# Seven half products for block 1's second product, with loads and neighbouring work moved

## The chip, the cores and the metric

The kernel runs on one core of one Trainium2 chip. A core has TensorE (PE in the profile; PEld is its weight load), VectorE (DVE), ScalarE (ACT), GpSimd (POOL) and SyncE (SP, which here only issues DMAs). Each engine runs its own instructions in program order and waits by semaphores for the others; SP, ACT and POOL can issue DMAs, in their own order too. The metric is the device time of one execution in microseconds (us); before the change the median of three runs is 279.38 us.

## What is computed

Linear attention over 8 batches, 8 heads, 576 positions and a head dimension of 64, with an RMS norm per head, and behind it a layer norm and a two-layer perceptron with a residual (512 to 2048 to 512):

```python
kv = np.einsum('bhsd,bhse->bhde', k, v)
out = np.einsum('bhsd,bhde->bhse', q, kv)
rms = np.sqrt(np.mean(out * out, axis=-1, keepdims=True) + 1e-06)
x = out / rms * g_norm                      # heads side by side: 512 columns
...
xn = (x - mu) / np.sqrt(var + 1e-06) * g_ln
ch = np.maximum(xn @ w_ch1, 0.0) @ w_ch2
return (x + ch).astype(np.float32)
```

Inputs and output are float32, the matrix products run in bfloat16.

## The kernel before

**Blocks and tiles.** Of each batch's 576 positions, 512 make one block of four tiles of 128 rows; the 64 left of each batch are gathered in a ninth block, "rem". For a block PE makes the first product (`mm1`, into `m1`, with ACT's ReLU from a PSUM bank of tag "p1", of which there are three) and then the second (`mm2`), which is scaled by the row's 1/std (`rstds`) and added to x. Blocks follow one another on PE without a break: mm1 and mm2 of block 0, of block 1, and so on.

**The attention of the next batch** is made in between. For batch b: `kv_of(b)` (40 small matmuls into the one PSUM bank of tag "misc", then two ACT copies); the turning of q, either by a DVE copy into `q_p` and a DMA transpose issued by SP (`turn_q_dma`), or in part by PE transposes through "misc" or "ops" banks and ACT copies (`turn_q`); and four tiles. `plan_tile` puts a tile's steps at given times: `first` is the product o (PE), its square (ACT) and the reduction over heads (DVE); `second` is the root (ACT), its inverse, y, x and the centred bfloat16 copy xc (all DVE); `turn` transposes xc, on PE (through "misc", with an ACT copy) or by a DMA transpose; `var` is the sum of squares on ACT.

**Time by hand.** `tick()` is called by the products, about once per 16 matmuls of 128 columns or 4 of 512, and runs what `at(slot, fn)` has put on the agenda for that tick, before the matmuls of the tick. So a slot sets the place of an instruction in the order of each engine's queue, not a time. A block has 16 ticks of mm1 and 16 of mm2, or 14 of mm2 if it is in `SEVEN`; slots are counted at 32 a block, and those in the second half of a block of `SEVEN` are pressed together by 14/16.

**Seven half products.** In the blocks of `SEVEN` (2 to 7 and "rem") `mm2_seven` makes the second product by Strassen's scheme in Winograd's form: rows, the 2048 inner elements (even and odd groups) and the columns are each halved, and seven products of halves with sums of halves take the place of eight. The sums of the weights' quarters, T1 to T4, are made once by DVE (slots 40 to 43); those of m1's quarters, S1 to S4, are made by DVE in each block as the ReLUs come in (`row_sums`), S3 in place. Each product is two ticks of eight matmuls with 256 columns. ACT scales results out of PSUM, DVE adds others (L558), and POOL adds float32 halves, x among them. Block 2 alone has its own order of products, and its mm1 handles two tiles at a time (256 columns); later blocks take four (512 columns).

**Blocks 0 and 1** make the second product straight, in 64 matmuls of 512 columns (L697). Block 0's is cut into parts of the inner dimension, because w2 is still arriving; for both, `finish` scales and adds by one DVE operation per tile (L706), and `store` issues the tile's two DMAs on SP (on POOL for tiles 2 and 3 of block 1). Block 1's mm1 runs tile by tile (128 columns).

**Loads** are issued by POOL, in program order: w1, w2[0:4] and [4:8] (128 rows each), batch 1's q, k and v in two DMAs each, the rest of w2, then, from slot 9.6, memsets and batch 2's k, v and q. The loads of a later batch reuse the buffers of the one before the last; POOL first copies one element of the turned q (`gate`), which makes it wait until that q has been read.

Of the kernel before, what the change touches and what calls it, by code (L numbers as in the profile page):

```python
# [14 lines left out]
def kernel(  # L15
# [11 lines left out]
    nc = tc.nc  # L27
# [19 lines left out]
    NB = 2  # L47
# [124 lines left out]
    load_w2(0, 4)  # L172
    load_w2(4, 8)
    for dst, src in ((q_in, q), (k_in, k), (v_in, v)):
        load(dst[1], src, 1)
    load_w2(8, 10)
    load_w2(10, 12)
    load_w2(12, nDe)

# [270 lines left out]

    def plan_tile(s, make, turn_at, on_pe, var_at):
        box = []

        def first():
            t = make()
            box.append(t)
            if t.mms:
                t.o()
            t.sq()
            t.red()  # L460

        def second():
            t = box[0]
            t.y()
            t.x()
            t.xc_w()

        at(s, first)
        at(s + 2, second)
        at(turn_at, lambda: box[0].turn(on_pe))  # L470
        at(var_at, lambda: box[0].var())
# [8 lines left out]

    SEVEN = {2, 3, 4, 5, 6, 7, "rem"}
    H2, C2 = nDe // 2, Dm // 2
    SPLIT = (0, 6, 12, nDe)
    SPLIT_2, TICKS_2 = (0, 12, nDe), ((0, 1, 4, 7), (0, 1, 4, 6))
    sums = {}

# [3 lines left out]
    def w2_q(odd, cols):  # L490
        return w2_sb[:, odd::2, cols * C2:cols * C2 + C2]

    B11, B12, B21, B22 = (w2_q(o, c) for o, c in ((0, 0), (0, 1), (1, 0), (1, 1)))
    weight_sums = (lambda: nc.vector.tensor_sub(T1, B12, B11),
                   lambda: nc.vector.tensor_sub(T3, B22, B12),
                   lambda: nc.vector.tensor_add(T2, T3, B11),
                   lambda: nc.vector.tensor_sub(T4, B21, T2))

# [40 lines left out]
    def mm2_seven(b):  # L539
# [22 lines left out]
        def p1():  # L562
            product(p_x, a11, b11, True, False)
            scaled(v0, p_x, 0)
            scaled(v1, p_x, 1)

        def p2():
            product(p_x, a12, b21, False, True)
            scaled(o(0, 0), p_x, 0)
            G.tensor_add(o(0, 0), o(0, 0), x(0, 0))  # L570

# [7 lines left out]
        def p4():  # L579
            product(p_q, a22, T4, True, True)  # L580
            scaled(q, p_q, 1)
            G.tensor_add(q, q, x(1, 0))  # L582

        def p5():
            product(p_z, S1, T1, True, False)
            scaled(r5, p_z, 1)
            G.tensor_add(r5, r5, x(1, 1))

        def p6():
            product(p_y, S2, T2, True, False)  # L590
            scaled_add(u2, p_y, 0, v0)
            G.tensor_add(u2, u2, x(0, 1))

        def p7():
# [3 lines left out]

        for p in ((p1, p4, p2, p5, p6, p7, p3) if b == 2 else (p1, p4, p6, p5, p2, p3, p7)):
            p()  # L600
# [64 lines left out]
    def mm1(b, t0, n, c0=0, c1=nDe):  # L665
# [3 lines left out]
        for de0 in range(c0, c1, per):  # L669
            tick()  # L670
            p1 = ps1.tile([128, per, n * 128], f32, tag="p1", name="p1")
            for i in range(per):
                de = de0 + i
                for kk in range(nK):
                    nc.tensor.matmul(p1[:, i, :], lhsT=w1_sb[:, kk, de * 128:(de + 1) * 128],  # L675
                                     rhs=blk[2][:, kk, sl],
                                     start=(kk == 0), stop=(kk == nK - 1))
            nc.scalar.activation(m1[:, de0:de0 + per, sl], p1, func=AF.Relu)  # L678
            del p1
            if b == 2 and t0 + n == 4 and de0 + per in SPLIT_2:  # L680
                i = SPLIT_2.index(de0 + per)
                row_sums(b, SPLIT_2[i - 1] // 2, SPLIT_2[i] // 2, TICKS_2[i - 1])
            elif b in SEVEN and b != 2 and de0 + 1 in SPLIT:
                i = SPLIT.index(de0 + 1)
                row_sums(b, SPLIT[i - 1] // 2, SPLIT[i] // 2, range(4))
# [16 lines left out]
    def finish(b, ts, p2):  # L702
        if ts % 2 == 0:
            o_pair[b] = outp.tile([128, 2, Dm], f32, tag="osb", name="o_sb")
        o_sb = o_pair[b][:, ts % 2]
        nc.vector.scalar_tensor_tensor(o_sb, in0=p2, scalar=rstds[b][:, ts:ts + 1],  # L706
                                       in1=blks[b][0][:, ts], op0=ALU.mult, op1=ALU.add)
        store(b, ts, o_pair[b][:, ts % 2:ts % 2 + 1])

    def store(b, ts, o_sb, c0=0, c1=Dm, upper=None):  # L710

        n = o_sb.shape[1]
        if b == "rem":
# [4 lines left out]
            return  # L718
        eng = nc.gpsimd if b == 1 and ts >= 2 else nc.sync
        for half in range(2):  # L720
# [155 lines left out]
    at(9.5, next_memsets)  # L876
    load_batches(9.6, (("k", 2), ("v", 2), ("q", 2)), lambda: ())
    at(11, lambda: t[3].turn(True))
# [4 lines left out]

    def q_start():
        q_ps[1] = kv_in.tile([128, JJ, H, D], bf16, tag="qp", bufs=1, name="q_p")
        nc.vector.tensor_copy(q_ps[1].rearrange("p j h d -> p h j d"), q_in[1])
        qts[1] = qt_pool.tile([128, JJ, HP, 128], bf16, tag="qt", name="qt")
        nc.sync.dma_start_transpose(
            qts[1][:, 2:].rearrange("p j hp t -> p (j hp) t"),
            q_ps[1][:, 2:].rearrange("p j h d -> p (j h d)"))  # L890

    def q_turns():
        turn_q(1, 0, ps_out, "ops")
        turn_q(1, 1, ps_m, "misc")
        del q_ps[1]

    at(14.5, q_start)
    at(19, q_turns)
    at(23, lambda: kv_of(1))
    for j, s, tn in ((0, 24, 30), (1, 27, 34), (2, 31, 38), (3, 35, 42)):  # L900
        plan_tile(s, lambda j=j: main_tile(1, j), tn, True, s + 6.7)
    at(36.2, lambda: keep_q(1))
    at(46, lambda: rstd_of(1))

    at(36, lambda: kv_of(2))
    at(36.9, lambda: turn_q_dma(2))
    for j, s, tn in ((0, 45, 51), (1, 49, 55), (2, 53, 61), (3, 57.5, 63)):
        plan_tile(s, lambda j=j: main_tile(2, j), tn, False, s + 6.7)
    at(58, lambda: keep_q(2))
    at(70, lambda: rstd_of(2))  # L910

# [4 lines left out]
    for slot, what, after in (  # L916
            (47, (("k", 3), ("v", 3), ("q", 3)), lambda: (turned_q(2),)),
            (68, (("q", 4), ("k", 4), ("v", 4)),
             lambda: (turned_q(3), blks[2][2][:1, nK - 1, 511:])),
            (92.7, (("q", 5), ("k", 5), ("v", 5)), lambda: (turned_q(4),)),  # L920
# [4 lines left out]

    for b, s in ((3, 56), (4, 93), (5, 123), (6, 155), (7, 187)):
        at(s, lambda b=b: kv_of(b))
# [14 lines left out]

    for b, at_q, at_o in ((3, 56.2, (66.9, 70.7, 74.5, 78.4)), (4, 81, (96.5, 102.7, 109, 115)),
                          *((b, 32 * b - 47.2, tuple(32 * b - i for i in (34.5, 27.3, 20.1, 12.9)))
# [6 lines left out]
    for i in range(nK):  # L951
        at(17 + i, lambda i=i: nc.vector.tensor_scalar_mul(w1_sb[:, i], w1_sb[:, i],
                                                           g_lnT_sb[:, i:i + 1]))
    for i, fn in enumerate(weight_sums):
        at(40 + i, fn)

# [5 lines left out]
    p2s += [ps2.tile([128, Dm], f32, tag="p2", name="p2") for _ in range(2)]  # L962
    for de0, de1 in ((0, 8), (8, 10), (10, 12)):
        for ts in range(4):
            mm2_part(0, ts, p2s[ts], de0, de1)
    for ts in range(4):
        p2 = p2s[ts]
        p2s[ts] = None
        mm2_part(0, ts, p2, nDe * 3 // 4, nDe)
        finish(0, ts, p2)  # L970
        del p2
    del blks[0], m1s[0]
    for ts in range(4):
        mm1(1, ts, 1)
    mm2(1)
# [38 lines left out]
```

## Time and profile before

| | us |
|---|---|
| median of 3 runs (279.3 to 279.63) | 279.38 |
| the profiled execution | 279.33 |
| its span, first to last instruction | 277.3 |
| PE busy | 269.2 |
| DVE busy | 195.9 |
| ACT busy | 179.5 |
| POOL busy | 101.7 |

The order of the first stages, by the first matmul of each in the chain of waits: block 0's mm1 at 14.83, its mm2 at 32.60, block 1's mm2 at 65.05, block 2's mm1 at 80.39, block 3's mm1 at 109.59; and in the timeline block 1's mm1 at 48.48 and block 2's mm2 at 95.14. From 150 to 200 PE is busy for all of the 50 us, and DVE for 35.6. In the chain of work that ended last PE has 82% of the span, DVE 8%, DMA 4%.

How to read the lines shown below: a line of the chain is start, duration, engine, operation and source line, with the number of instructions merged; a line of a timeline is the same with the shapes, and in brackets how long the engine stood idle before it and what released it; a line of waits is who waited for whom, the total, how often, and the longest. A window's line is start and end, and then for each engine the busy time and the number of instructions.

### The profile page before, as it was taken

What the parts mean: (1) busy time and instruction counts of PE and PEld (TensorE: products, weight loads), DVE (VectorE), ACT (ScalarE), POOL (GpSimd) and SP (SyncE); (2) the same over time, 40 slices, a digit from 0 to 9 for tenths busy, and PEclk for the clock granted to TensorE, in tenths of its full rate; (3) what the DMA queues carried; (4) which work ended last, traced back from release to release, by engine and by line L of the source; (5) the groups of instructions that cost most, each with busy time, mean ns of one, the idle gap of its engine ahead of it and who ended that gap; (6) DMA issues with size and microseconds to landing.
All of it is one profiled execution on the core that took longest, in us unless ns stands there. A gap on an engine that the chain in (4) does not pass through costs nothing.

```text
span 277.3 us, 6629 instructions
## 1 busy us (share of the span) xinstructions
PE 269.2 (97%) x2614; PEld 189.6 (68%) x2614; DVE 195.9 (71%) x446; ACT 179.5 (65%) x398; POOL 101.7 (37%) x127
## 2 busy tenths in 40 slices
PE   8899999999999999999999999999999999999994
PEld 3589855996569886458845874597458745874683
DVE  6676438897966898899569856985797469923564
ACT  3567754796448783777677767776777487846610
POOL 8522770025034256701870187017201800180141
PEclk9999999999999999999999999999999999999999
DMA  7999999959995994995499639991611061105032
GB/s 215 199 207 205 200 197 190 260 106 144 189 183 84 199 126 92 216 227 98 41 185 239 134 26 178 245 134 21 161 28 21 20 163 29 21 20 151 2 76 76
DMA packets 65366, 36.80 MB, mean 133 GB/s; under 512 B 35120, under 2 KB 62004, under 8 KB 65336
## 3 DMA queue, kind: packets, MB, share of 16 engines
q0 software_dynamic: 28736, 18.29, 46.4%
q1 hardware_dynamic: 36008, 17.12, 30.4%
q10 hardware_dynamic: 592, 0.98, 1.0%
q8 instruction: 20, 0.33, 0.5%
q14 instruction: 10, 0.08, 0.1%
HBM read 36.71 MB, written 9.44 MB: 166 GB/s over the span
## 4 chain that ended last, share of the span: by engine, by line
PE 82%; DVE 8%; DMA 4%; ACT 3%; issue 1%; POOL 1%; DVEq 0%; POOLq 0%
PE p L675 42%; PE p L697 8%; PE p_y L519 7%; PE p_z L519 7%; PE p_x L519 6%; PE p_s L519 4%; DMA w_sb<-in_moe_w_ch_dram 4%; PE p_q L519 3%; PE o_ps L298 2%; PE kv_ps L271 2%; DVE S L509 1%; DVE ss L375 1%; DVE x_blk L397 1%; DVE o_ps L379 1%; DVE S L508 1%
## 5 line engine op out<-in xcount | busy, mean ns | idle before, releaser
L675 PE MATMUL p<-xT_blk,w_sb 128*128 128x128 bf16 (+2 forms) x1024 | 131.5, 286 | 0.6 <-DMA w_sb<-in_moe_w_ch_dram 0.4
L678 ACT ACTIVATE m<-p 128x512 bf16<-128x512 f32 x144 | 85.5, 597 | 38.9 <-PE p L675 36.2
L675 PEld LDWEIGHTS <-w_sb 128*128 128x128 bf16 x1024 | 78.7, 98 | 45.0 <-issue 0.7
L519 PEld LDWEIGHTS <-m 128*128 128x128 bf16 x448 | 43.3, 98 | 6.5
L375 DVE TENSOR_REDUCE ss<-sq 128x8 f32<-128x512 f32 x35 | 23.8, 680 | 28.7 <-ACT sq L304 28.6
L582 POOL TENSOR_TENSOR q<-q,x_blk 128x512 f32<-128x512 f32 x6 | 8.1, 1348 | 83.1 <-ACT q L553 83.1
L519 PEld LDWEIGHTS <-S 128*128 128x128 bf16 x344 | 32.8, 98 | 4.8 <-DVE S L509 1.1
L697 PE MATMUL p<-w_sb,m 128*128 128x512 bf16 x128 | 29.6, 379 | 0.0
L415 ACT ACTIVATE dev<-x_blk,st_blk 128x512 f32<-128x512 f32 x36 | 25.8, 718 | 1.4 <-DVE st_blk L401 1.4
L379 DVE TENSOR_TENSOR o_ps<-o_ps,inv 128x512 f32<-128x512 f32 x33 | 23.1, 700 | 3.1
L304 ACT ACTIVATE sq<-o_ps 128x512 f32<-128x512 f32 x35 | 20.8, 595 | 5.0 <-PE o_ps L298 5.0
L397 DVE SCALAR_TENSOR_TENSOR x_blk<-o_ps,g_norm_sb 128x512 f32<-128x512 f32 x33 | 22.8, 691 | 1.1
L519 PE MATMUL p_x<-w_sb,m 128*128 128x256 bf16 x192 | 23.4, 273 | 0.0
L697 PEld LDWEIGHTS <-m 128*128 128x128 bf16 x128 | 12.0, 98 | 12.3
L383 ACT ACTIVATE rms<-ss,eps_sb 128x8 f32<-128x8 f32 x36 | 10.7, 297 | 12.6 <-DVE ss L375 12.2
L507 DVE TENSOR_TENSOR S<-m 128x768 bf16<-128x768 bf16 (+2 forms) x20 | 10.7, 536 | 11.4 <-ACT m L678 11.4
L422 DVE TENSOR_SCALAR xc<-x_blk,st_blk 128x512 bf16<-128x512 f32 x32 | 17.7, 553 | 1.1
L558 DVE SCALAR_TENSOR_TENSOR u<-p_y,rstd,v 128x256 f32<-128x256 f32 x24 | 10.4, 476 | 5.0 <-PE p_y L519 5.0
L509 DVE TENSOR_TENSOR S<-m,S 128x768 bf16<-128x768 bf16 (+2 forms) x20 | 12.6, 634 | 0.4
L553 ACT ACTIVATE v<-p_x,rstd 128x256 f32<-128x256 f32 x24 | 9.4, 475 | 5.0 <-PE p_x L519 5.0
L390 DVE RECIPROCAL inv<-rms 128x8 f32<-128x8 f32 x36 | 7.1, 197 | 7.6 <-ACT rms L383 7.3
L519 PE MATMUL p_z<-w_sb,S 128*128 128x256 bf16 x96 | 11.8, 273 | 0.6 <-DVE S L509 0.6
(143 smaller groups left out, 347.6 us busy)
## 6 DMA issues: line engine op xcount, KB each, us to landing
out_dram<-o_sb SPq DMA_DIRECT2D x24, 256.0 KB, 6.1
w_sb<-in_moe_w_ch_dram POOLq DMA_DIRECT2D x7, 512.0 KB, 13.5
q_in<-in_q_dram POOLq DMA_DIRECT2D x7, 320.0 KB, 5.2
k_in<-in_k_dram POOLq DMA_DIRECT2D x7, 320.0 KB, 7.8
v_in<-in_v_dram POOLq DMA_DIRECT2D x7, 320.0 KB, 11.1
q_in<-in_q_dram POOLq DMA_DIRECT2D x8, 256.0 KB, 8.2
out_dram<-o_sb SPq DMA_DIRECT2D x16, 128.0 KB, 4.6
k_in<-in_k_dram POOLq DMA_DIRECT2D x7, 256.0 KB, 8.7
```

The source lines that it names most:

```text
L304: nc.scalar.activation(self.sq_t, self.o_ps, func=AF.Square)
L375: nc.vector.tensor_reduce(self.ss, self.sq_t, axis=AX.X, op=ALU.add)
L379: nc.vector.tensor_mul(self.o_ps, self.o_ps, self.inv().to_broadcast([128, H, D]))
L383: nc.scalar.activation(self.r, self.ss, func=AF.Sqrt, scale=1.0 / D, bias=eps_sb)
L397: nc.vector.scalar_tensor_tensor(x_blk[:, ts].rearrange("p (h d) -> p h d", h=H), in0=self.o_ps, scalar=1.0, in1=g_norm_sb.to_broadcast([1 ...
L415: nc.scalar.activation(dev, x_blk[:, ts], func=AF.Square, bias=st[:, 1, ts:ts + 1], accum_out=st[:, 2, ts:ts + 1])
L422: nc.vector.tensor_scalar_add(self.xc_t, x_blk[:, self.ts], st[:, 1, self.ts:self.ts + 1])
L509: lambda: nc.vector.tensor_sub(S4, a12, S2),
L519: nc.tensor.matmul(dst[:, t - ts[0], :c1 - c0], lhsT=a[:, i, t * 128:(t + 1) * 128], rhs=w[:, i, c0:c1], start=start and t == ts[0] and i ...
L675: nc.tensor.matmul(p1[:, i, :], lhsT=w1_sb[:, kk, de * 128:(de + 1) * 128], rhs=blk[2][:, kk, sl], start=(kk == 0), stop=(kk == nK - 1))
L678: nc.scalar.activation(m1[:, de0:de0 + per, sl], p1, func=AF.Relu)
L697: nc.tensor.matmul(p2[:, c0:c1], lhsT=m1s[b][:, de, ts * 128:(ts + 1) * 128], rhs=w2_sb[:, de, c0:c1], start=(de == 0), stop=(de == nDe - 1))
```

## The change

Block 1 joins `SEVEN`, with block 2's order of products and two-tile groups for its tiles 2 and 3 in mm1. In blocks 1 and 2 three of POOL's additions are put behind that of u2. Block 1's row sums get their own ticks.

The weights' sums are cut into four calls of four operations on 512 columns, one at slot 13 and three at 34.5 to 39. w2 is loaded in pairs behind w2[0:4], and batch 1's q and k go ahead of them, its v behind the first pair; block 0's parts follow the pairs. Batch 2's q is loaded ahead of its k and v. Block 0's outputs are scaled by ACT and added by POOL, and their stores are issued by POOL at slot 40.2. Batch 1's attention steps come one to three slots earlier, batch 2's q is partly turned on PE, its tile 3 too, and slots of batches 2 and 3 and the loads of 3 and 4 move; batch 4's loads no longer wait for block 2's last transposed tile.

```diff
     load_w2(0, 4)
-    load_w2(4, 8)
-    for dst, src in ((q_in, q), (k_in, k), (v_in, v)):
-        load(dst[1], src, 1)
-    load_w2(8, 10)
-    load_w2(10, 12)
-    load_w2(12, nDe)
+    load(q_in[1], q, 1)
+    load(k_in[1], k, 1)
+    load_w2(4, 6)
+    load(v_in[1], v, 1)
+    for de in range(6, nDe, 2):
+        load_w2(de, de + 2)
...
-    def plan_tile(s, make, turn_at, on_pe, var_at):
+    def plan_tile(s, make, turn_at, on_pe, var_at, second_at=None):
...
-        at(s + 2, second)
+        at(second_at or s + 2, second)
...
-    SEVEN = {2, 3, 4, 5, 6, 7, "rem"}
+    SEVEN = {1, 2, 3, 4, 5, 6, 7, "rem"}
...
+    TICKS_1 = ((1, 2, 4, 7), (0, 1, 2, 5))
...
-    weight_sums = (lambda: nc.vector.tensor_sub(T1, B12, B11),
-                   lambda: nc.vector.tensor_sub(T3, B22, B12),
-                   lambda: nc.vector.tensor_add(T2, T3, B11),
-                   lambda: nc.vector.tensor_sub(T4, B21, T2))
+    def weight_sums(i0, i1):
+        i = slice(i0, i1)
+        t1, t2, t3, t4, b11, b12, b21, b22 = (w[:, i] for w in (T1, T2, T3, T4, B11, B12, B21, B22))
+        nc.vector.tensor_sub(t3, b22, b12)
+        nc.vector.tensor_add(t2, t3, b11)
+        nc.vector.tensor_sub(t4, b21, t2)
+        nc.vector.tensor_sub(t1, b12, b11)
...
+        late = []
+
+        def add(dst, a, c):
+            if b in (1, 2):
+                late.append(lambda: G.tensor_add(dst, a, c))
+            else:
+                G.tensor_add(dst, a, c)
...
-            G.tensor_add(o(0, 0), o(0, 0), x(0, 0))
+            add(o(0, 0), o(0, 0), x(0, 0))
...
-            G.tensor_add(q, q, x(1, 0))
+            add(q, q, x(1, 0))
...
-            G.tensor_add(r5, r5, x(1, 1))
+            add(r5, r5, x(1, 1))
...
             G.tensor_add(u2, u2, x(0, 1))
+            while late:
+                late.pop(1 if len(late) == 3 else 0)()
...
-        for p in ((p1, p4, p2, p5, p6, p7, p3) if b == 2 else (p1, p4, p6, p5, p2, p3, p7)):
+        for p in ((p1, p4, p2, p5, p6, p7, p3) if b in (1, 2) else (p1, p4, p6, p5, p2, p3, p7)):
...
-            if b == 2 and t0 + n == 4 and de0 + per in SPLIT_2:
+            if b in (1, 2) and t0 + n == 4 and de0 + per in SPLIT_2:
                 i = SPLIT_2.index(de0 + per)
-                row_sums(b, SPLIT_2[i - 1] // 2, SPLIT_2[i] // 2, TICKS_2[i - 1])
-            elif b in SEVEN and b != 2 and de0 + 1 in SPLIT:
+                row_sums(b, SPLIT_2[i - 1] // 2, SPLIT_2[i] // 2, (TICKS_1 if b == 1 else TICKS_2)[i - 1])
+            elif b in SEVEN and b not in (1, 2) and de0 + 1 in SPLIT:
...
-        nc.vector.scalar_tensor_tensor(o_sb, in0=p2, scalar=rstds[b][:, ts:ts + 1],
-                                       in1=blks[b][0][:, ts], op0=ALU.mult, op1=ALU.add)
-        store(b, ts, o_pair[b][:, ts % 2:ts % 2 + 1])
+        r, x = rstds[b][:, ts:ts + 1], blks[b][0][:, ts]
+        nc.scalar.activation(o_sb, p2, func=AF.Copy, scale=r)
+        nc.gpsimd.tensor_add(o_sb, o_sb, x)
+        o_tile = o_pair[b][:, ts % 2:ts % 2 + 1]
+        at(40.2, lambda: store(b, ts, o_tile))
...
-        eng = nc.gpsimd if b == 1 and ts >= 2 else nc.sync
+        eng = nc.gpsimd if b == 0 or b == 1 and ts >= 2 else nc.sync
...
-    load_batches(9.6, (("k", 2), ("v", 2), ("q", 2)), lambda: ())
+    load_batches(9.6, (("q", 2), ("k", 2), ("v", 2)), lambda: ())
...
-    at(14.5, q_start)
-    at(19, q_turns)
-    at(23, lambda: kv_of(1))
-    for j, s, tn in ((0, 24, 30), (1, 27, 34), (2, 31, 38), (3, 35, 42)):
-        plan_tile(s, lambda j=j: main_tile(1, j), tn, True, s + 6.7)
-    at(36.2, lambda: keep_q(1))
+    at(12.5, lambda: q_start(1, 2))
+    at(17, lambda: q_turns(1, (ps_out, "ops"), (ps_m, "misc")))
+    at(22, lambda: kv_of(1))
+    for j, s, tn in ((0, 23, 28.6), (1, 26, 33), (2, 29, 37), (3, 32, 39)):
+        plan_tile(s, lambda j=j: main_tile(1, j), tn, True, (27.7, 41, 43, 45)[j])
+    at(33.2, lambda: keep_q(1))
...
-    at(36, lambda: kv_of(2))
-    at(36.9, lambda: turn_q_dma(2))
-    for j, s, tn in ((0, 45, 51), (1, 49, 55), (2, 53, 61), (3, 57.5, 63)):
-        plan_tile(s, lambda j=j: main_tile(2, j), tn, False, s + 6.7)
-    at(58, lambda: keep_q(2))
-    at(70, lambda: rstd_of(2))
+    at(40, lambda: kv_of(2))
+    at(29.5, lambda: q_start(2, 1))
+    at(35, lambda: q_turns(2, (ps_m, "misc")))
+    for j, s, x_at, tn, va in ((0, 42, 44, 46, 55.5), (1, 44.2, 46.2, 49, 57.5),
+                               (2, 55.5, 59.5, 61, 63), (3, 60.5, 62.6, 70, 67.5)):
+        plan_tile(s, lambda j=j: main_tile(2, j), tn, j == 3, va, x_at)
+    at(61, lambda: keep_q(2))
+    at(70.5, lambda: rstd_of(2))
...
-            (47, (("k", 3), ("v", 3), ("q", 3)), lambda: (turned_q(2),)),
-            (68, (("q", 4), ("k", 4), ("v", 4)),
-             lambda: (turned_q(3), blks[2][2][:1, nK - 1, 511:])),
+            (43, (("q", 3), ("k", 3), ("v", 3)), lambda: (turned_q(2),)),
+            (61.5, (("q", 4), ("k", 4), ("v", 4)), lambda: (turned_q(3),)),
...
-    for b, s in ((3, 56), (4, 93), (5, 123), (6, 155), (7, 187)):
+    for b, s in ((3, 62.5), (4, 93), (5, 123), (6, 155), (7, 187)):
...
-    for b, at_q, at_o in ((3, 56.2, (66.9, 70.7, 74.5, 78.4)), (4, 81, (96.5, 102.7, 109, 115)),
+    for b, at_q, at_o in ((3, 52, (68.5, 72.5, 76.5, 83)), (4, 81, (96.5, 102.7, 109, 115)),
...
-    for i, fn in enumerate(weight_sums):
-        at(40 + i, fn)
+    for i0, i1, slot in ((0, 2, 13), (2, 4, 34.5), (4, 6, 37), (6, 8, 39)):
+        at(slot, lambda i0=i0, i1=i1: weight_sums(i0, i1))
...
-    for de0, de1 in ((0, 8), (8, 10), (10, 12)):
+    for de0, de1 in ((0, 4), (4, 6), (6, 8), (8, 10), (10, 12), (12, 14)):
         for ts in range(4):
             mm2_part(0, ts, p2s[ts], de0, de1)
...
-        mm2_part(0, ts, p2, nDe * 3 // 4, nDe)
+        mm2_part(0, ts, p2, 14, nDe)
         finish(0, ts, p2)
...
-    for ts in range(4):
-        mm1(1, ts, 1)
+    mm1(1, 0, 1)
+    mm1(1, 1, 1)
+    mm1(1, 2, 2)
     mm2(1)
```

`q_start(b, j0)` and `q_turns(b, ...)` are the old `q_start` and `q_turns` with the batch as an argument: `q_start` copies q to `q_p` on DVE and turns the groups from j0 on by a DMA transpose, `q_turns` turns the others on PE.

## Prediction

> **What bounds the kernel now.** I read the page's busy times first, then the waits of PE, the chain of waits, the busy times by stretches of five microseconds, and the timelines of DVE, ACT and POOL around block 1.
>
> ```profile
> PE 269.2 (97%) x2614; PEld 189.6 (68%) x2614; DVE 195.9 (71%) x446; ACT 179.5 (65%) x398; POOL 101.7 (37%) x127
> ```
>
> PE is busy for 97%, and the slices show its clock at 9 throughout. What PE no longer has to do is gained, unless PE then waits. It waits very little now:
>
> ```profile
> PE p_z L519 <- DVE S L509: 0.6, 1, 0.6
> PE p L675 <- DMA w_sb<-in_moe_w_ch_dram: 0.4, 1, 0.4
> ```
>
> The first of these is block 2's seventh row sum. In the chain:
>
> ```profile
> 102.07 3.36 DVE S L509 x2
> 105.43 0.04 issue
> 105.47 0.39 PE p_z L519 x2
> 105.87 0.75 PE kv_ps L271 x40
> ```
>
> The other side is DVE around block 1 (columns PE, PEld, DVE, ACT, POOL, clock, DMA share, GB/s; of 5 us each): 4.86, 4.17 and 4.68 are busy, ACT up to 4.84, and POOL is idle.
>
> ```profile
> 45.00:50.00 5.00, 5.00 (x51) 3.34 (x50) 4.86 (x11) 2.52 (x6) 0.40 (x1) 1.00 1.42 194
> 50.00:55.00 5.00, 4.93 (x115) 4.82 (x113) 4.17 (x10) 4.41 (x12) 0.00 (x0) 1.00 1.25 287
> 55.00:60.00 5.00, 5.00 (x93) 5.00 (x91) 4.68 (x9) 4.84 (x12) 0.00 (x0) 1.00 0.68 143
> ```
>
> **PE's own sum.** Second product of block 1: the chain has 28 matmuls of L697 in 6.04 us, 0.216 each, 64 make 13.80. A half product (16 of L519) is 1.75 us, seven make 12.25: **-1.55**. First product: row groups 2 and 3 go together. 64 matmuls of 128 columns take 3.57 us (0.0558 each), 32 of 256 columns 3.49 (0.109): 128 of the one, 7.14, become 64 of the other, 6.98: **-0.16**. Added: four transposes for q of batch 2 and four for its tile 3, 0.22 each (L429 x4): **+0.44**. The o products and kv products only move. Block 2's wait: **-0.58**, see below. Sum **-1.85**.
>
> **Loads.** In the timeline of POOL every load issue waits for the landing of the eighth load before it:
>
> ```profile
> 23.43 0.68 POOL L98 DMA_DIRECT2D v_in<-in_v_dram  x1 [1.94 <-DMA w_sb<-in_moe_w_ch_dram]
> 25.95 0.71 POOL L119 DMA_DIRECT2D w_sb<-in_moe_w_ch_dram  x1 [1.84 <-DMA w_sb<-in_moe_w_ch_dram]
> 28.44 0.71 POOL L119 DMA_DIRECT2D w_sb<-in_moe_w_ch_dram  x1 [1.78 <-DMA w_sb<-in_moe_w_ch_dram]
> 30.26 0.76 POOL L119 DMA_DIRECT2D w_sb<-in_moe_w_ch_dram  x1 [1.11 <-DMA q_in<-in_q_dram]
> ```
>
> So the last quarter of w1 landed at 23.4, w2[0:4] at 25.9, w2[4:8] at 28.4: 512 KB per 2.55 us. In the new order that rate gives q1 28.8, k1 31.7, w2[4:6] 32.9, v1 35.8, w2[6:8] 37.1, then each pair 1.27 later, the last at 42.2. Needs, with tick 16 at 32.60 (first L697), 0.8625 a tick and what lies between: w2[4:6] 36.5, v1 38.2 (tick 22), w2[6:8] 39.0, w2[8:10] 40.9. The thinnest slack is 1.9 us; I take 0. Gone, it costs what is late, one for one; the bound is -0 to +1, as qt's transpose (4.37 us on SP) shares the DMA engines. Two more w2 issues (0.75 each) put POOL's memsets and batch 2's six issues 1.4 us later, to 36.4; q2, now first of them, lands at 45, k2 and v2 by 51 (kv of batch 2 is at 57). The eight stores of block 0 leave SP, which has only transposes there, for POOL: 0.54 each (1.63 for three in block 1), 4.3 us from tick 40 (56.7). Batch 3's gate stands behind them at 61.2, against 61.0 now. Batch 4's gate comes at 75 instead of 83, so its copy waits for nothing.
>
> **DVE.** Block 0's outputs (L706, 0.74, every 0.66) leave it: -2.6 us before 51.4. The weight sums become 16 operations of 512 columns: such a row sum takes 0.42 and the next starts 0.45 later, so 1.8 us a call; four calls 7.2 instead of 4 x 1.24 = 5.0. The first call is at tick 13, where DVE idles now (4.21 us), the others after tile 3 of batch 1. Block 1's row sums add 0.87 and 0.33 (spacings in the chain) four times, 4.8 us, and six L558 of 0.43 replace four L706. So DVE has no gap between 44 and 74:
>
> Tile 1 of batch 1 ends its xc at 48.78 now. Its tile 0 comes a tick (0.86) earlier and one L706 less stands before it: 47.75. Reduce of tile 2, 0.65: 48.4. Copy of q2, 0.82: 49.2. Inverse to xc of tile 2, 2.4 (46.40 to 48.78 for tile 1 now): 51.6. Reduce of tile 3: 52.25. ACT's root behind it, 0.30, stands in ACT's queue at tick 34 ahead of the ReLUs of ticks 34 on and the copy of q2's transposes; with 0.60 and 0.57 these end at 53.7. PE wants the one "misc" bank again at tick 37: 32.60 + 16 x 0.8625 + 5 x 0.89 + 0.45 + 0.75 + seven times 0.22 = 53.6. So there is **no slack left**: what delays DVE between 48 and 53 delays PE one for one, through ACT. Behind it, the last part of S1 would end at 70.1, and the product that reads it starts at 70.3; S2, S4 and S3 have 2 us and more. At the end of block 1, POOL's six additions (1.27 each) now run beside the xc of batch 2's tiles 2 and 3. With one wait of 0.75 for each of these the last ends at 83.7, and PE turns it at tick 68, 84.7: nothing reaches PE; without that slack, up to +0.7.
>
> **ACT and POOL for block 0's outputs.** ACT gets four copies (0.60) at 47.4 to 49.9, two of them behind tile 2's root. Three of batch 1's variances (0.71) leave the ticks up to 40 for 41 to 45, which makes up for them, and the ten scalings of block 1's halves (0.475) fall in ticks without a ReLU: 0 for ACT by itself; were PE to wait for one such copy, +0.6. POOL gets four additions of 1.27 to 1.35 (L582, L575) from about 48.0 to 53.2. This is where a price is unknown:
>
> ```profile
> 112.89 1.34 POOL L575 TENSOR_TENSOR o_sb<-u,q 128x512 f32<-128x512 f32 x1
> 114.12 1.33 POOL L576 TENSOR_TENSOR o_sb<-u,r 128x512 f32<-128x512 f32 x1
> 114.14 1.61 DVE L422 TENSOR_SCALAR xc<-x_blk,st_blk 128x512 bf16<-128x512 f32 x1
> 31.29 2.35 DVE L886 COPY q_p<-q_in 128x2560 bf16<-128x2560 bf16 x1 [4.21 <-DMA q_in<-in_q_dram]
> ```
>
> xc has a median of 0.49, here it takes 1.61 under POOL additions: +1.12. The copy of q takes 0.82, under POOL's memsets 2.35. No row has the copy under an addition. In the new order it is ready at 48.4 and the first addition starts at 48.0. Two DVE operations can meet POOL there: the copy (to 49.3, +0.9) and tile 2's xc (+0.75, the rest of the third addition). Bounds: 0 if DVE comes first, 1.65 with both. A small lead of either engine decides, so I take one wait of the middle size, **+0.85**. The Trainium skill ("SBUF — State Buffer", section "Who interferes with whom") says that DVE and GpSimd share a port pair as an exclusive lock and that whoever issues first blocks the other for the whole instruction. By that rule both would wait here, and the sum would be -0.2; the trace has it for xc, not for the copy.
>
> **Block 2.** Its row sums ran beside POOL's additions (L508 on 512 columns 1.49 instead of 0.42, the two L509 3.42 instead of 0.87 + 0.33). These additions now come after u's, when the sums are done; also u's no longer stands behind three others. Tile 3 of batch 3 comes later, and adds about 3 us to DVE there. From tick 76 the sums and tiles need 7.9 us to the end of S4, which is read 12 ticks (10.5 us) later; the wait of 0.58 goes. If not, +0.58.
>
> Total: -1.85 + 0.85 = **-1.0**. The profiled execution took 279.33 with a span of 277.3, so 2.03 lie around it; the median is 279.38. I predict 276.3 for the span and **278.4** for the median.
>
> **Rivals.** (1) DVE gets in ahead of POOL, or the waits end in slack: 279.38 - 1.85 = 277.5. For it: the two are 0.4 us apart; against: POOL is busy for five microseconds without a break. (2) Both waits count in full: -0.2, 279.2. (3) DVE's unbroken stretch is the bound: S1's last part comes a microsecond late, because the copy of q3 or the weight sums are slowed, and the fourth product waits: 279.4. For it: 0.2 us of slack; against: PE's stalls before it widen that slack. (4) **Slower**: q2 lands late. Its copy is at the head of DVE's queue at 48.4, tiles 2 and 3 of batch 1, ACT's root and the ReLUs behind it stand still, and PE with them. Each microsecond after 48.4 costs one; from 50.3 on the gain of 1.85 is eaten. Now q2 lands at 55.1; less k2 and v2, 2.9 us each, it would be 49.3; if the transposes and the later issue hold it to 51.3, the time is 279.38 - 1.85 + 2.9 = 280.4. Against it: 5 us of block 0's stores ran beside these loads and no longer do, which leads to 45.
>
> **How the numbers follow.** Forecast 0.40, rival (1) 0.25, (2) 0.15, (3) 0.08, (4) 0.12. About 0.2%, 0.56 us, is what a measurement of this kernel tells from no change: faster is below 278.82, slower above 279.94. The forecast (but for 0.05 of it), (1) and a part of (3) are faster: 0.64; (2), most of (3) and that 0.05: 0.24; (4): 0.12. The range runs from (1) less the spread of the small terms, 277.4, over (2) and (3) to the edge of (4), 279.7. The forecast's own range is 277.9 to 278.9.
>
> **What would show it.** PE's matmuls of 512 columns in the second product fall from 128 to 64, and 112 half-width ones are added. The wait of PE for S is gone. Right: the copy of q2 or an xc between 48 and 54 has more than 1 us beside a POOL addition, and PE waits some 0.9 us for ACT near 54. Wrong: PE busy without a gap there (rival 1); DVE idle before the copy of q2, released by its DMA (4); PE waiting at 39 for w2 or v; a new wait of PE for S near 70 (3). The forecast falls if the additions beside DVE cost nothing, or if PE's waits go over 2 us.

## The result and the profile after

The changed kernel takes **281.44 us** (median of six runs, 280.84 to 281.7) against 279.51 for the kernel before in the same comparison: ratio 1.0067, 95% interval 1.0056 to 1.0078, so 0.67% slower. The profiled execution took 280.84 with a span of 278.7 (279.33 and 277.3 before).

PE has less work than before and waits more. First the busy line of the page, then the list of what PE waited for (who waited for whom: total, times, longest):

```profile
PE 268.7 (96%) x2606; PEld 194.4 (70%) x2606; DVE 199.9 (72%) x464; ACT 185.6 (67%) x414; POOL 118.0 (42%) x144
```

```profile
PE tp L429 <- ACT qt L190: 1.0, 1, 1.0
PE kv_ps L271 <- DMA v_in<-in_v_dram: 0.8, 1, 0.8
...
PE p_y L523 <- DVE S L512: 0.6, 1, 0.6
PE p L712 <- DMA w_sb<-in_moe_w_ch_dram: 0.5, 1, 0.5
```

Block 2's old wait of 0.58 for S has left the list. Four waits of 0.5 us and more are new, in three places. The timeline of PE shows where:

```profile
39.05 0.82 PE L271 MATMUL kv_ps<-v_in,k_in 128*64 128x64 bf16 x40 [0.82 <-DMA v_in<-in_v_dram]
40.42 1.02 PE L712 MATMUL p<-w_sb,m 128*128 128x512 bf16 x4 [0.55 <-DMA w_sb<-in_moe_w_ch_dram]
...
56.24 0.38 PE L429 MATMUL tp<-identity,xc 128*128 128x128 bf16 x4 [1.00 <-ACT qt L190]
...
129.27 1.26 PE L523 MATMUL p_y<-T,S 128*128 128x256 bf16 x10 [0.60 <-DVE S L512]
```

From such timelines come the starts of the stages, and from these their lengths (us). The last column is the best kernel of the experiments, e15.

| stage, to the start of the next | before | after | e15 |
|---|---|---|---|
| start of block 0's second product | 32.44 | 32.43 | 32.43 |
| block 0, second product | 16.04 | 17.73 | 17.04 |
| block 1, first product | 16.41 | 17.61 | 17.17 |
| block 1, second product | 15.34 | 13.70 | 13.69 |
| block 2 | 29.20 | 28.40 | 28.40 |
| block 3, to the o product at 134.38 (before), 135.59, 133.68 | 24.95 | 25.72 | 24.95 |
| the rest of the span | 142.9 | 143.1 | 143.2 |

Block 1's second product and block 2 give 2.44 us. Blocks 0 and 1 lose 2.89 ahead of that, of which 2.37 are three of the waits and the rest transposes and o products that moved there, and block 3 loses 0.77, of which 0.60 is the wait for S. The sum is +1.4 in the span.

**Loads.** The answer of the DMA view for the stretch from 34 to 40 us (queue and kind: packets, MB, share of 16 engines' time; q0 has the loads, q1 the transpose of batch 1's q). Before:

```profile
q0 software_dynamic: 1442, 1.08, 116.4%
q1 hardware_dynamic: 362, 0.09, 11.4%
```

After:

```profile
q0 software_dynamic: 892, 0.71, 88.7%
q1 hardware_dynamic: 888, 0.23, 46.2%
```

In the same six microseconds 0.37 MB less is loaded, and the transpose's packets have 46% of the DMA engines' time for 0.23 MB. At the 1.08 MB per 6 us of before, 0.37 MB is 2.1 us of loading. SP's issue of this transpose takes 4.09 us from 29.54 on (4.37 from 33.66 before), but q1's share, window by window, is 2.6% from 28 to 34, 42.8% and 64.8% from 34 to 38, 31.1% from 38 to 40, 30.5% and 25.8% in the next two stretches of 2 us, and 0.1% only from 44 on: the transfer lasts until about 44. Before, it had 3.9% from 36 to 38, and its bulk ran from 38 to 46, when v of batch 1 and w2[6:8] had landed; now it falls among them.

Sharing is not all of it. The windows from 36 to 38 (PE, PEld, DVE, ACT, POOL; clock, DMA share, GB/s), before and after:

```profile
36.00:38.00 2.00, 2.00 (x11) 0.89 (x10) 1.19 (x3) 1.20 (x4) 2.00 (x3) 1.00 1.26 205
36.00:38.00 2.00, 2.00 (x11) 0.79 (x9) 1.50 (x3) 1.30 (x5) 2.00 (x3) 1.00 1.53 102
```

Loads and transpose together move 102 GB/s there instead of 205, which is some 0.2 MB less in these two microseconds: from 36.5 to 37.3 the DMA engines nearly stand still (more on it in the last section). So of the 0.37 MB, 0.14 are bytes that the transpose moves more than before, and the standstill has most of the rest; this split is an estimate from these rows.

**DVE beside POOL** (timelines of DVE and POOL, after):

```profile
49.76 1.87 DVE L904 COPY q_p<-q_in 128x2560 bf16<-128x2560 bf16 x1
...
53.50 0.80 DVE L422 TENSOR_SCALAR xc<-x_blk,st_blk 128x512 bf16<-128x512 f32 x1
```

```profile
49.67 5.75 POOL L723 TENSOR_TENSOR o_sb<-o_sb,x_blk 128x512 f32<-128x512 f32 x4 [5.16 <-DVE xc L422]
```

The first of POOL's four additions starts 0.09 ahead of the copy of q2. The copy takes 1.87 instead of 0.82, xc 0.80 instead of 0.49, and ACT and PE follow: the wait of 1.00 at 56.24.

**Block 3.** The two last of block 2's postponed additions (POOL), and a row sum of block 3 (DVE) beside them:

```profile
116.47 1.60 POOL L588 TENSOR_TENSOR o_sb<-u,q 128x512 f32<-128x512 f32 x1
118.04 1.57 POOL L589 TENSOR_TENSOR o_sb<-u,r 128x512 f32<-128x512 f32 x1
```

```profile
118.53 1.50 DVE L513 TENSOR_TENSOR S<-m,S 128x768 bf16<-128x768 bf16 x1
```

Such a sum takes 0.55 elsewhere. POOL comes to these additions at 116.47 only, because its gate and the six issues of batch 5's loads (112.28 to 116.5) stand ahead of them.

### The profile page after: what moved, and what is told of

The parts are those of the page before. It is cut to its first block, busy times and chain, and to the rows that moved or that the text cites. A ratio compares the mean times of both kernels' runs of the same rounds, so it can differ in the third digit from the quotient of the medians.

```text
span 278.7 us, 6646 instructions
## 1 busy us (share of the span) xinstructions
PE 268.7 (96%) x2606; PEld 194.4 (70%) x2606; DVE 199.9 (72%) x464; ACT 185.6 (67%) x414; POOL 118.0 (42%) x144
## 4 chain that ended last, share of the span: by engine, by line
PE 73%; DMA 14%; DVE 9%; ACT 2%; issue 1%; POOL 0%; DVEq 0%; POOLq 0%
PE p L690 35%; DMA w_sb<-in_moe_w_ch_dram 11%; PE p_z L523 9%; PE p_y L523 9%; PE p_x L523 8%; PE p_s L523 4%; PE p_q L523 4%; DMA v_in<-in_v_dram 3%; PE o_ps L298 2%; PE kv_ps L271 2%; DVE ss L375 1%; DVE o_ps L379 1%; DVE x_blk L397 1%; DVE xc L422 1%; DVE S L513 1%
## 5 line engine op out<-in xcount | busy, mean ns | idle before, releaser
L523 PEld LDWEIGHTS <-m 128*128 128x128 bf16 x512 | 49.4, 98 | 7.3 <-issue 0.2
L523 PEld LDWEIGHTS <-S 128*128 128x128 bf16 x392 | 37.5, 98 | 5.1 <-DVE S L512 0.9
L578 POOL TENSOR_TENSOR q<-q,x_blk 128x512 f32<-128x512 f32 x5 | 6.4, 1288 | 70.0 <-ACT q L557 70.0
L523 PE MATMUL p_x<-w_sb,m 128*128 128x256 bf16 x224 | 27.3, 273 | 0.0
L605 POOL TENSOR_TENSOR u<-u,x_blk 128x512 f32<-128x512 f32 x7 | 8.9, 1266 | 40.8 <-DVE u L562 40.8
L511 DVE TENSOR_TENSOR S<-m 128x768 bf16<-128x768 bf16 (+2 forms) x22 | 12.5, 569 | 12.2 <-ACT m L693 12.2
L562 DVE SCALAR_TENSOR_TENSOR u<-p_y,rstd,v 128x256 f32<-128x256 f32 x28 | 12.2, 475 | 5.3 <-PE p_y L523 5.3
L712 PE MATMUL p<-w_sb,m 128*128 128x512 bf16 x64 | 15.0, 379 | 0.5 <-DMA w_sb<-in_moe_w_ch_dram 0.5
L523 PE MATMUL p_y<-T,S 128*128 128x256 bf16 x112 | 13.5, 273 | 0.6 <-DVE S L512 0.6
L523 PE MATMUL p_y<-T,m 128*128 128x256 bf16 x112 | 13.9, 273 | 0.0
L523 PE MATMUL p_z<-w_sb,S 128*128 128x256 bf16 x112 | 13.5, 273 | 0.0
## 6 DMA issues: line engine op xcount, KB each, us to landing
w_sb<-in_moe_w_ch_dram POOLq DMA_DIRECT2D x5, 512.0 KB, 13.5
```

Of the source, the lines that this page charges most:

```text
L511: for i, fn in enumerate((lambda: nc.vector.tensor_add(S1, a21, a22), lambda: nc.vector.tensor_sub(S2, S1, a11), lambda: nc.vector.tensor_ ...
L523: nc.tensor.matmul(dst[:, t - ts[0], :c1 - c0], lhsT=a[:, i, t * 128:(t + 1) * 128], rhs=w[:, i, c0:c1], start=start and t == ts[0] and i ...
L562: V.scalar_tensor_tensor(dst[:, t], in0=src[:, t], scalar=rstd[:, 2 * rows + t:2 * rows + t + 1], in1=other[:, t], op0=ALU.mult, op1=ALU.add)
L712: nc.tensor.matmul(p2[:, c0:c1], lhsT=m1s[b][:, de, ts * 128:(ts + 1) * 128], rhs=w2_sb[:, de, c0:c1], start=(de == 0), stop=(de == nDe - 1))
```

## The experiments

The theories, as the expectations name them: **A**, the DMA transpose of batch 1's q takes DMA time that v and w2 need, and so makes PE wait at 38 to 40. Its rival **B**: only the order of v and w2's pairs is wrong. **C**, the wait for ACT at 56 comes from POOL's additions, which hold DVE's copy of q2 and xc up; its rival **D**: DVE's own work is too long there. **E**, the wait for S in block 3 comes from batch 5's loads standing ahead of POOL's postponed additions. All are edits of the changed kernel; a line `...` in an edit stands for lines left out. Times are compared with runs of the kernel before on the same chip (279.35 to 279.49).

**e1: batch 1's transpose issued later** (37.7 instead of 29.5; copy and transpose of groups 2 on move from slot 12.5 to 19.5).

```diff
-    at(12.5, lambda: q_start(1, 2))
-    at(17, lambda: q_turns(1, (ps_out, "ops"), (ps_m, "misc")))
...
+    at(12.5, lambda: q_first(1, 2))
+    at(17, lambda: q_turns_kept(1, (ps_out, "ops"), (ps_m, "misc")))
+    at(19.5, lambda: q_rest(1, 2))
```

`q_first` and `q_rest` are the two parts of `q_start`, and `q_turns_kept` is `q_turns` without the `del`.

> Only batch 1's DMA transpose of q is put later: q's first two groups are copied at slot 12.5 as in the changed kernel, the other three at slot 19.5 behind three of w1's scalings, so that the transpose starts near 37.5 us and not at 29.5. Theory A (the transpose shares the DMA engines with the loads and holds up v1 and w2[6:8]): PE's waits for v (0.82) and for w2 (0.55) vanish, v1 lands by 36.5, and the time falls from 281.4 by 1.4 to 280.0. Rival B (the order of the loads and the pairs of w2 make them late): both waits stay within 0.3 us, 281.4. If the transposed q itself comes late now, PE waits for it at the third o product of batch 1 near 46 us.

Measured 284.32, ratio 1.0173 (1.0155 to 1.019). The waits for v and w2 are gone, as A says. But the transposed q is late by more than was saved (PE's timeline):

```profile
49.35 0.61 PE L298 MATMUL o_ps<-kv_pack,qt 128*128 128x128 bf16 x4 [3.56 <-DMA qt<-q_p]
```

From the issue at 37.7 it takes 11.6 us to land beside batch 2's loads. Issued this late the transpose costs more than it saved.

**e2: v of batch 1 ahead of w2[4:6].**

```diff
-    load_w2(4, 6)
-    load(v_in[1], v, 1)
-    for de in range(6, nDe, 2):
+    load(v_in[1], v, 1)
+    for de in range(4, nDe, 2):
```

> Only the load order is changed: batch 1's v goes ahead of the pair w2[4:6]. Rival B (v stands behind the pair): v1 lands 1.3 us earlier, the wait for v goes, the wait for w2 does not grow: 280.6. Theory A (all loads together are late by the transpose's share of the DMA engines): the bytes up to w2[6:8] are the same, so what the wait for v loses the wait for w2 gains; their sum stays 1.2 to 1.5 us and the time at 281.4.

281.41, ratio 1.0064 (1.0044 to 1.0083): no change. The wait for v is gone, and the one for w2 is 1.23, nearly as long as the two were together (PE's timeline):

```profile
37.83 1.89 PE L711 MATMUL p<-w_sb,m 128*128 128x512 bf16 x8 [1.23 <-DMA w_sb<-in_moe_w_ch_dram]
```

The sum of what is loaded by then decides, not the order: B falls.

**e9: batch 1's q turned wholly on PE**, without the DMA transpose: twelve more transposes on PE, 0.66 us by the 0.22 for four.

```diff
-        nc.sync.dma_start_transpose(
+        if j0 < JJ:
+            nc.sync.dma_start_transpose(
...
-    at(12.5, lambda: q_start(1, 2))
-    at(17, lambda: q_turns(1, (ps_out, "ops"), (ps_m, "misc")))
+    at(12.5, lambda: q_start(1, JJ))
+    at(17, lambda: turn_q(1, 0, ps_out, "ops"))
+    at(17.1, lambda: turn_q(1, 1, ps_m, "misc"))
+    at(18, lambda: turn_q(1, 2, ps_out, "ops"))
+    at(19, lambda: turn_q(1, 3, ps_m, "misc"))
+    at(20, lambda: (turn_q(1, J, ps_out, "ops"), q_ps.pop(1)))
```

> Batch 1's q is turned wholly on PE: twelve more transposes and three more ACT copies at slots 18 to 20, and no DMA transpose in front of the loads. Theory A (DMA supply up to 47 us is the bound, and the transpose takes some 4 us of it): PE's waits for v (0.82) and w2 (0.55) and for a late transposed q all go; PE has 0.66 us more; time 281.4 - 1.37 + 0.66 = 280.7, and less spread. Rival G (the loads alone are too late for a schedule that asks for them 1 to 2 ticks earlier): the waits stay above 0.5 in sum and the time rises to 281.8.

280.30, ratio 1.0032 (1.0021 to 1.0043). Both waits are gone, and the DMA view from 34 to 40 has the loads alone, at 1.20 MB instead of 0.71:

```profile
q0 software_dynamic: 1382, 1.20, 125.2%
```

So it is the transpose that makes PE wait, by its bytes and by the standstill that comes with it. Without it the loads come as the prediction had estimated: v's second half lands 12.7 us after its issue at 23.50, at 36.2 (35.8 was estimated), and q2's 7.8 us after 37.48, at 45.3 (45). In the changed kernel it is 15.3 us after 23.41 and 10.6 after 38.45: 38.7 and 49.05. What is left of PE's new waits is 1.0 for ACT and 0.6 for S.

**e4: POOL's additions at slot 40.1**, one by one ahead of the stores.

```diff
-        nc.gpsimd.tensor_add(o_sb, o_sb, x)
+        at(40.1, lambda: nc.gpsimd.tensor_add(o_sb, o_sb, x))
```

> Only the four POOL additions of block 0's outputs are moved, from right behind ACT's scalings to slot 40.1, just ahead of their stores. Theory C (the additions block DVE's copy of q2 and xc of tile 2, and this reaches PE by ACT's root): the copy takes 0.82 and not 1.87, xc 0.49 and not 0.80, PE's wait for ACT before tile 2's turn goes from 1.0 to below 0.1, time 280.4. Rival D (DVE's own work is too long there, whatever POOL does): the wait stays above 0.6, 281.2. The additions then meet the weight sums near 58 to 62, which nothing needs before 68.

281.52, ratio 1.007 (1.0053 to 1.0086). The additions ran at 49.72, as before the edit: a slot sets the place in POOL's queue, and nothing stood in between. It tells nothing about C.

**e10: the additions behind batch 3's loads in POOL's queue** (slot 43.5, the stores at 43.6).

```diff
-        nc.gpsimd.tensor_add(o_sb, o_sb, x)
+        at(43.5, lambda: nc.gpsimd.tensor_add(o_sb, o_sb, x))
-        at(40.2, lambda: store(b, ts, o_tile))
+        at(43.6, lambda: store(b, ts, o_tile))
```

> Block 0's four POOL additions and its stores are put behind the loads of batch 3 in POOL's queue (slot 43.5), whose first instruction waits for batch 2's turned q; so they run near 60 us, and not at 49.7 as in the changed kernel and in the trial with slot 40.1, where nothing held POOL up. Theory C: the copy of q2 takes 0.82 and not 1.87, xc of tile 2 0.49 and not 0.80, PE's wait for ACT falls from 1.0 to below 0.1, time 280.4. Rival D (DVE's own work is too long there): the wait stays above 0.6, 281.2.

284.5, ratio 1.0176 (1.016 to 1.0193). The copy takes 0.82, xc 0.48, and PE's wait at 56 is gone: C holds. The additions now meet a sum of weights instead (DVE, then POOL, then PE):

```profile
62.80 4.20 DVE L501 TENSOR_TENSOR T<-w_sb 128x512 bf16<-128x512 bf16 x1
```

```profile
62.93 5.19 POOL L724 TENSOR_TENSOR o_sb<-o_sb,x_blk 128x512 f32<-128x512 f32 x4
```

```profile
68.95 1.05 PE L690 MATMUL p<-xT_blk,w_sb 128*128 128x256 bf16 x8 [2.05 <-ACT m L693]
```

Such a sum takes 0.42 alone. Behind it in DVE's queue are tile 2's reduction, on ACT its root and the ReLUs, and PE.

**e5: block 0's outputs back on DVE** by one operation a tile, as before the change (the stores as in the changed kernel).

```diff
-        nc.scalar.activation(o_sb, p2, func=AF.Copy, scale=r)
-        nc.gpsimd.tensor_add(o_sb, o_sb, x)
+        nc.vector.scalar_tensor_tensor(o_sb, in0=p2, scalar=rstds[b][:, ts:ts + 1],
+                                       in1=blks[b][0][:, ts], op0=ALU.mult, op1=ALU.add)
```

> Block 0's outputs go back to DVE (four operations of 0.74, one each 0.66) and leave ACT and POOL; their stores stay on POOL at slot 40.2. Theory C's price of the move was 1.05 + 0.31 us of blocked DVE, DVE's own work for it 2.64: PE's wait for ACT grows from 1.0 to about 2.3, time 282.7. If POOL's additions cost DVE more than its own work would, the wait falls below 1.0.

283.63, ratio 1.0145 (1.0129 to 1.016). The wait for ACT (PE's waits) is 2.2. So the additions on POOL cost 1.0, and the alternative on DVE costs more: the four operations of 0.7 stand in the same queue.

**e12: the copy of q2 a slot earlier** (28.5 instead of 29.5), ahead of tile 2's reduction and so ahead of POOL's first addition.

> Only DVE's copy of q2 is moved, from behind the reduction of batch 1's tile 2 to ahead of it (slot 28.5 instead of 29.5), 0.6 us earlier, so that it starts before POOL's first addition of block 0's outputs. Theory C (who starts first keeps the other waiting): the copy takes 0.82 and not 1.87, PE's wait for ACT before tile 2's turn falls from 1.0 to 0.1 or less, time 281.4 - 0.9 = 280.5; the loads' waits stay. Rival (the next operation, xc of tile 2, takes over the wait): the wait stays above 0.5, 281.0.

282.32, ratio 1.0108 (1.0072 to 1.0143). With batch 1's DMA transpose still there, q2 has not landed when the copy's turn comes (DVE, then PE):

```profile
50.42 1.58 DVE L904 COPY q_p<-q_in 128x2560 bf16<-128x2560 bf16 x1 [0.80 <-DMA q_in<-in_q_dram]
```

```profile
55.59 0.38 PE L187 MATMUL tp<-identity,q_p 128*128 128x128 bf16 x4 [1.99 <-ACT xT_blk L431]
```

The copy waits 0.80, starts behind POOL's addition after all, and PE waits 1.99. This is the mechanism of the prediction's rival (4), at the head of DVE's queue; in the changed kernel itself q2 lands in time, but at 49.05 only 0.7 us ahead of its copy. So e12 doesn't show what the copy costs when it goes first.

**e6: batch 5's loads behind the additions** (slot 96.5 instead of 92.7).

```diff
-            (92.7, (("q", 5), ("k", 5), ("v", 5)), lambda: (turned_q(4),)),
+            (96.5, (("q", 5), ("k", 5), ("v", 5)), lambda: (turned_q(4),)),
```

> Only the loads of batch 5 are put behind block 2's last two POOL additions (slot 96.5 instead of 92.7). Theory E (block 2's postponed additions and then the loads push the last two additions onto block 3's row sums): the additions run some 4 us earlier, the row sums at 116 to 120 take 0.55 each, and PE's wait of 0.60 for S in block 3 goes, time 280.8. Rival F (block 3's row sums are late because DVE starts the block late): the wait stays at 0.4 or more, 281.4.

281.77, ratio 1.0086 (1.0059 to 1.0113), no gain. The wait for S is gone and the row sums take 0.55 again, as E says. In its place (PE's waits):

```profile
PE o_ps L298 <- DMA qt<-q_p: 0.5, 1, 0.5
```

Block 3's part is 25.60 long, 25.72 in the changed kernel and 24.95 before: batch 5's q now comes too late.

**e11: e9, e10 and e6 together.**

> Batch 1's q on PE, block 0's additions behind batch 3's loads, and batch 5's loads behind block 2's last additions, together. If theories A, C and E hold and their prices add, the time is 281.4 - 1.37 + 0.66 - 1.0 - 0.6 = 279.1, at or just below the kernel before; of PE's waits only those of the first 15 us and some 0.3 for ACT remain. If the waits move on to another place, it stays above 280.

284.0, ratio 1.0161 (1.0137 to 1.0185): the additions are behind the loads as in e10, and PE's wait there is 3.1.

**e13 and e14: e9, e6, and the copy of q2 at slot 28.5 (e13) or 27.5 (e14).**

> Batch 1's q turned wholly on PE, the copy of q2 one slot earlier, and batch 5's loads behind block 2's last additions. Theories A, C and E: the waits for v, w2 and S go, the one for ACT falls to 0.1; from the 280.3 of q on PE alone, 280.3 - 0.9 - 0.6 = 278.8, 0.6 below the kernel before. If the waits move on to another place it stays at 279.5 or above.

> The same with the copy of q2 at slot 27.5, ahead of tile 1's inverse, where DVE waits 0.3 us for ACT anyway. If q2 has landed by 46 us, DVE is 0.3 us ahead at tile 3 and the time is 278.5; if it has not, DVE stands at the head of its queue until it has, and the time rises one for one above 278.8.

279.91, ratio 1.0018 (1.0009 to 1.0026), and 279.89, ratio 1.0024 (1.001 to 1.0038). Both are still some 0.2% slower than the kernel before. Without batch 1's transpose q2 has landed by then, the copy goes ahead of POOL and takes 0.82, and the wait of 1.0 shrinks to 0.3 (0.4 in e14). It doesn't go, because now xc meets the additions: it takes 0.95 in e13 and 1.26 in e14, 0.49 alone. At the start of block 3's first product e13 is 0.62 ahead of the kernel before (108.81 against 109.43). It loses that again by the end, 0.41 of it to the late q of batch 5:

```profile
134.33 0.40 PE L298 MATMUL o_ps<-kv_pack,qt 128*128 128x128 bf16 x4 [0.41 <-DMA qt<-q_p]
```

**e15: e13 with batch 5's loads parted**: q where it was, k and v behind the additions.

```diff
-            (96.5, (("q", 5), ("k", 5), ("v", 5)), lambda: (turned_q(4),)),
+            ((92.7, 96.5, 96.5), (("q", 5), ("k", 5), ("v", 5)), lambda: (turned_q(4),)),
```

> Batch 1's q turned wholly on PE and the copy of batch 2's q at slot 28.5, as in the two runs before; of batch 5's loads q keeps its place (slot 92.7), k and v go to 96.5, behind block 2's two last additions. Theory E (in block 3 two of block 2's postponed float32 additions on POOL run beside a row sum on DVE because POOL was blocked by these loads; and q of batch 5, not k and v, is what comes late when all three are postponed): no wait of PE for S in block 3 (0.6 in the changed kernel) and the wait of the o product at 134 for the transposed q (0.4 to 0.8 when all three go late) is 0.1 or less; time 279.3, some 0.6 less than with all three late, which is level with the kernel before. Rival: the two additions still meet the row sum, as q's two issues and the gate alone hold POOL up: wait for S 0.5, time 279.9, no gain. Second rival: DMA traffic, not the place of the issue, sets when q lands: wait for q stays, 279.9.

**279.04** (278.95 to 279.39, twelve runs), the kernel before 279.42: ratio 0.9984 (0.9976 to 0.9993). It is 0.16% faster than the kernel before, with the interval clear of 1 but less than the 0.2% that the prediction takes as the least to be told from no change, and about 0.8% faster than the changed kernel by the two ratios. POOL's order, from its timeline, and all that PE still waits for:

```profile
111.25 0.71 POOL L97 DMA_DIRECT2D q_in<-in_q_dram  x1
111.95 0.71 POOL L98 DMA_DIRECT2D q_in<-in_q_dram  x1
112.65 1.30 POOL L588 TENSOR_TENSOR o_sb<-u,q 128x512 f32<-128x512 f32 x1
113.88 1.48 POOL L589 TENSOR_TENSOR o_sb<-u,r 128x512 f32<-128x512 f32 x1
115.32 0.70 POOL L97 DMA_DIRECT2D k_in<-in_k_dram  x1
```

```profile
PE p L214 <- DVE eps_sb L150: 1.3, 1, 1.3
PE tp L187 <- ACT xT_blk L431: 0.3, 1, 0.3
PE p L690 <- DMA w_sb<-in_moe_w_ch_dram: 0.3, 1, 0.3
```

The first of these (1.3) is at the kernel's start and in the kernel before too. The additions are over at 115.36, before the row sums that they had held up; one of the earlier row sums still takes 1.04, and no one waits for it.

## Why the prediction was wrong

The forecast was 278.4 with a range to 279.7; the kernel is slower, and the range doesn't hold it.

- **The step that failed is the one on the loads**: "The thinnest slack is 1.9 us; I take 0", with a bound of "-0 to +1, as qt's transpose (4.37 us on SP) shares the DMA engines". PE waits 0.82 for v and 0.55 for w2[6:8]: **+1.37**, past the bound. v is there for PE at 39.05; 35.8 was the estimate. The loads alone were estimated rightly (36.2 for v in e9); the price of the transpose beside them was not. The 4.37 us is the time of the issue, not of the transfer, and the loads' rate came from a stretch without a transpose. This much could be read from the trace of before: from 38 to 40 the transpose moves 0.08 MB in 30.4% of the time, and the transposed q lands at 47.16, 13.5 us after the issue. The standstill could not: the trace of before has none. Experiments e1 and e9 show the step twice: without the transpose in that stretch both waits go. From the same step q2 lands 4 us later than the estimated 45.
- **The second miss is in block 3, +0.77**, not in the sum at all. "These additions now come after u's, when the sums are done" is right for block 2, whose wait of 0.58 is gone (its part is 0.80 shorter). But POOL's queue was not walked on to its end: four additions and batch 5's six issues stand ahead of the last two, which so reach block 3's row sums. e6 and e15 show the cause of the wait, 0.60 of the 0.77.
- **Right in place and size, not in the count of waits: the price of POOL beside DVE.** "+0.85" was taken, PE waited 1.00, for ACT, at 56.24; "near 54" was the place, and PE was itself 1.4 late by then. But the forecast had one wait, and both operations waited, as in rival (2): the copy lost 1.05 and xc 0.31, 1.36 of the 1.65 at which (2) counts them, and 1.00 of it reached PE. That it came near 0.85 is in part luck. The rule of the Trainium skill that the prediction set beside it ("SBUF — State Buffer", "Who interferes with whom": who issues first blocks the other) agrees with this trace for the copy as well: 1.87 behind an addition, 0.82 in e13 and e15, where it goes first. e10's sum of weights does not fit it (see the last section).
- **Right: PE's own sum.** Second product -1.55: the stage is 1.64 shorter, with 64 matmuls of 512 columns gone. The first product's -0.16 and the transposes' +0.44 can't be seen apart from the o products that moved between stages.
- **Rivals.** No wait for S near 70: (3) doesn't occur. (4) doesn't occur in the changed kernel, by 0.7 us, only in e12. Of (2) the mechanism occurred, both waits, but not its price in full. None of the four has the loads of block 0 as its mechanism, although "PE waiting at 39 for w2 or v" was named as what would show the prediction wrong.

The sum with what was measured: -1.0 + 1.37 (loads) + 0.15 (1.00 instead of 0.85) + 0.77 (block 3) = +1.29; the span grew by 1.4. The profiled execution, 280.84, is the fastest of its six runs; why the median lies 0.6 above it no trace shows, and it stays open.

The saving itself is there: in e15 block 1's second product and block 2 are as much shorter as in the changed kernel (13.69 and 28.40), and the costs that remain are 0.66 for the twelve transposes that PE makes in place of the DMA engines (three times four at 0.22), a wait of 0.33 for ACT, and the moved steps.

## What to carry to other kernels

A transfer in the background has a price in DMA time: read from the DMA view what share it takes and what the loads beside it lose, rather than the duration of its issue, and expect that it can cost more in the stretch it is moved into, as the standstill did here. When work on a queue is postponed, follow that queue until it is empty, past the stage in question: the gain in block 2 came back as a loss in block 3. Where DVE and POOL are to meet, look at which operation starts first: the copy ahead of the additions took 0.82 and not 1.87, though the next operation, xc, then met them.

## What was not expected of the hardware

**The clock.** How long PE waits doesn't by itself decide whether the granted clock falls. It stayed at 1.00 through waits of 1.00 in the changed kernel, 1.99 in e12 and 2.19 in e5; it fell to 0.50 with the 3.56 of e1, the 3.07 of e11 and the 2.05 of e10. Windows of e1 around its wait from 45.8 to 49.35 (start and end; PE, PEld, DVE, ACT, POOL; clock, DMA share, GB/s):

```profile
46.00:48.00 2.00, 0.00 (x0) 0.00 (x0) 1.65 (x5) 0.00 (x0) 0.00 (x0) 0.97 1.31 187
48.00:50.00 2.00, 0.65 (x5) 0.56 (x6) 0.00 (x0) 0.00 (x0) 0.00 (x0) 0.50 1.40 193
```

The 0.97 says that the clock fell shortly before 48, some 2.1 us into the wait. It stays at 0.50 for some five microseconds after work resumes, so e1's wait of 3.56 cost, by estimate, some 2.7 us more than itself (half of 49.35 to 54.7). The Trainium skill ("TensorE: Matmul & The Clock Gate", "Part 1: The HAM clock gate") puts the fall to half the clock at one idle window of about 3.4 us. The trace doesn't agree that so much idle time must go before the fall: it was 2.1 us in e1, and in e10 the wait of 2.05 that ended at 68.95, with 0.9 us of work behind it:

```profile
70.00:72.00 2.00, 1.86 (x9) 1.28 (x9) 1.61 (x5) 1.19 (x5) 2.00 (x5) 0.50 1.07 296
```

Here the measurement decides: two microseconds can be enough, and need not be. The low clock lasted 3.4 us in e10 and e11 and 6.8 in e1. What sets e10's 2.05 apart from e5's 2.19 no run shows.

**How long DVE is held.** In e10 the sum of weights was held for 4.20 us, over about three of POOL's four additions, while the copy of q2 in the changed kernel came through after one (1.87). Both stood beside four additions in a row. By the records the sum starts 0.13 us ahead of the first addition, so going first didn't help it. What makes the difference was not tried.

**A standstill in the DMA.** In the changed kernel the transpose's stretch has some 0.8 us, 36.5 to 37.3, in which the DMA engines move about 10 to 15 GB/s instead of some 200. All six other runs in which this transpose is issued at about 30 (e2, e4, e5, e6, e10, e12) have such a stretch of 0.7 to 1.0 us between 35.8 and 38.2. None is there before the change (issue at 33.66), in e1 (37.7), or in the five runs without the transpose (e9, e11, e13, e14 and e15). So it belongs to the transpose at this place; what holds the engines there is open.
